# Three pairs of output blocks by seven products in steps 17 and 18 of an mLSTM and FFN kernel

## The chip, the cores and the metric

The kernel runs on one core of one Trainium2 chip, in f32 throughout. The metric is the device time of one execution in microseconds; lower is better. The engines are named as in the profile: PE (TensorE, matmul), PEld (TensorE's weight load), DVE (VectorE), ACT (ScalarE), POOL (GpSimd) and SP (SyncE, which issues most DMAs).

## The reference

An mLSTM cell runs over 768 time steps for 4 batches and 8 heads of 40; its output, as 3072 tokens of 320, goes through a multiplicative FFN:

```python
# cell, per time step t
C = f_stab * C + i_stab * outer(vt, kt);  n = f_stab * n + i_stab * kt
y[t] = sigmoid(o_gate[t]) * (C @ qt) / max(abs(n . qt), 1)
# FFN on x = y as (3072, 320)
a = x @ w1                  # 320 x 1024
b = x @ w2
out = ((a * b) @ w3) @ w_out   # 1024 x 1024, 1024 x 320
```

## The kernel before, in words

**Tiles.** The cell is computed in 24 units of 128 time steps of one batch: unit n is chunk n // 4 of batch n % 4. Four units (one chunk of all batches) make a token group of 512 tokens, six groups in all. The two last weights are folded once into one, w3 @ w_out, kept in `w3o` (128 x 8 x 320); `w3_mm` does this in eight parts ("wp" in the profile), called by `fold`. Their factors pass through `raw`, `w3` and `w3T` buffers and `wo`. After the fold, the memory of `wo` serves as `aside`.

**The FFN's first products** give `ab`, the product of x @ w1 and x @ w2, turned, 128 x 8 x 256 for each half group; six such tiles rotate. Groups 0 to 2 use the plain form (`up`, `up_rest`). Groups 3 to 5 use seven products where a 2 x 2 split of the matrices needs eight (`up_by_seven`, L676): it works on sums of weights (`weight_sums`, L659, four 128x512 operations on POOL for each of w1 and w2, into `raw` buffers) and sums of tokens (`token_sums`, L669, four 128x256 operations on DVE into a `w3T` buffer), keeps partial results in `aside`, and has POOL add and multiply.

**The FFN's last product** gives the output, 128 tokens by 320 a block, 24 blocks in all. The plain form (`ffn_out`, L741) takes 8 products of 320 columns a block. The form by seven (`out_by_seven`, L780) takes two blocks, a pair: 7 x 4 products of 160 columns, on four sums of `ab` (`ab_sums`, L771, four 128x512 operations on DVE) and four sums of the folded weight (`out_weight_sums`, L756, four 128x640 operations on POOL). Its results `p15`, `p67`, `p23` and `p4` are put together by one ACT copy and five DVE additions (L797 to L805). In the profile the products are "po" (or "cell", x32 or x16, where `ffn_out` borrows cell banks in steps 19 to 24) for the plain form and "o" for the form by seven. PE splits each f32 product in two instructions.

**The order** is written out in one loop over 32 steps (L828). Step s does, in this order: DMAs of later units' inputs on SP; the first decay of the state and the doubling of y's last columns (`twice`) on POOL; `fold`; products of `up_by_seven`; `weights(s + 1)` and `out_gate(s)` on ACT (steps 16 to 23); plain output blocks (L883 to L887); products of `up`; then `quarter_work`, the cell's own PE work, which finishes unit s - 1 and starts unit s ("cell" rows x128); then, on DVE, `x_turn` (from step 17 on: a unit's y is written to DRAM by `send` and read back by `get_back`) and `turn(s + 1)` (keys and queries turned by DVE), and on ACT `shift(s + 1)`; then `weighted` and `masks` of the next unit on POOL. Each engine works through its own instructions in the order in which they are written. Matmul results rotate through four PSUM banks of tag "m", so that a product that takes a bank waits until the engine that reads the bank's former result is through.

How much of the FFN each step does is set by lists: `n_down` (L818) says how many plain output blocks a step takes from `downs` (L812), `n_seven` how many parts of `up_by_seven` (one in each of steps 19 to 30), `n_out` how many pairs by seven (five, from step 27 on). In the kernel before, 14 blocks are plain: two in each of steps 16 to 20 and one in each of steps 21 to 24. `weight_sums` stands at the end of steps 15 and 16 (L988), the token sums of group 3 at the end of DVE's work in step 17 (L953), and the sums of the folded weight in steps 24 and 25 (L941), after the cell.

Of the kernel before, what the change touches and what calls it, by code (L numbers as in the profile page):

```python
# [8 lines left out]
FP = mybir.dt.float32  # L9
U32 = mybir.dt.uint32  # L10
AF = mybir.ActivationFunctionType
OP = mybir.AluOpType
# [4 lines left out]
def kernel(  # L17
# [26 lines left out]
    nc = tc.nc  # L44

    B, H, S, D = q.shape
    L = 64
    P = 128
    NT = S // L
    NT2 = S // P  # L50
    NU = NT2 * B
# [3 lines left out]
    DM = H * D  # L55
    BH = B * H
    DFF = moe_w1.shape[1]
    FO = DFF // P
    KF = DM // P
    REM = DM - KF * P  # L60
    GT = B
    TG = GT * P
    NG = NU // GT

    const = ctx.enter_context(tc.tile_pool(name="const", bufs=1))
    wst = ctx.enter_context(tc.tile_pool(name="wst", bufs=2))
    io = ctx.enter_context(tc.tile_pool(name="io", bufs=3))
# [42 lines left out]
    q_all = const.tile([P, NBQ * H * DP], FP, name="q_all")  # L110
    qbuf = [q_all[:, i * H * DP:(i + 1) * H * DP].rearrange("p (h d) -> p h d", d=DP) for i in range(NBQ)]
    kbuf = [const.tile([P, H, DP], FP, name=f"kbuf{i}") for i in range(NB)]
    v_all = const.tile([P, NBV * H * D1], FP, name="v_all")
# [9 lines left out]
    NY = 15  # L123
    KC = KF + 1
# [50 lines left out]
    CW = 512  # L175
# [79 lines left out]
    def fold():  # L255
        while ready_w3:
            w3_mm(ready_w3.pop(0))
        ready_w3.extend(turned_w3)
        turned_w3.clear()
# [11 lines left out]
    def out_gate(n):  # L271
        nc.scalar.activation(out=o_t[n], in_=o_t[n], func=AF.Tanh, scale=0.5)
# [27 lines left out]
    def weights(n):  # L300
        c, b = divmod(n, B)
        src = weights_tile(n) if n else spread(n)
        pw = weights_tile(n)
        for h in range(H):
            nc.scalar.activation(out=pw[:, h, :], in_=src[:, h, :], func=AF.Exp, bias=aT[:, c, b * H + h:b * H + h + 1])  # L305

    def masks(n):
        pw = weights_tile(n)
        for r in halves:
            nc.gpsimd.affine_select(out=pw[r], in_=pw[r], compare_op=OP.is_ge, fill=0.0, base=0,  # L310
                                    pattern=[[0, H], [1, L]], channel_multiplier=-1)
# [347 lines left out]
    def weight_sums(j):  # L659

        mem = [wst.tile([128, CW, 2], U32, name="raw", tag="raw", bufs=4).rearrange("p n two -> p (n two)").bitcast(FP)
               for _ in range(2)]
        S1, S2, S3, S4 = S_t[j] = [m[:, i * CW:(i + 1) * CW] for m in mem for i in range(2)]
        (A11, A21), (A12, A22) = ([(w1, w2)[j][:, cc, i * CW:(i + 1) * CW] for i in range(2)] for cc in range(KF))
        for dst, p, q, op in ((S1, A21, A22, OP.add), (S2, S1, A11, OP.subtract), (S3, A11, A21, OP.subtract),
                              (S4, A12, S2, OP.subtract)):
            nc.gpsimd.tensor_tensor(out=dst, in0=p, in1=q, op=op)

    def token_sums(gr):  # L669
        mem = wst.tile([128, FO, 128], FP, name="w3T", tag="w3T").rearrange("p k c -> p (k c)")  # L670
        T1, T2, T3, T4 = T_t[gr] = [mem[:, i * TH:(i + 1) * TH] for i in range(4)]
        (B11, B12), (B21, B22) = ([x_t[gr][:, cc, i * TH:(i + 1) * TH] for i in range(2)] for cc in range(KF))
        for dst, p, q in ((T1, B12, B11), (T2, B22, T1), (T3, B22, B12), (T4, B21, T2)):
            nc.vector.tensor_tensor(out=dst, in0=p, in1=q, op=OP.subtract)

    def up_by_seven(gr, f, bank, aside_by):  # L676

# [75 lines left out]

    KH, NH = FO // 2, DM // 2

    def out_weight_sums():  # L756

        T_o.extend(m[:, i * KH * NH:(i + 1) * KH * NH].rearrange("p (f n) -> p f n", n=NH)
                   for m, i in ((v_all, 0), (gates, 0), (gates, 1), (q_all, 0)))
        (B11, B12), (B21, B22) = ([w3o[:, k * KH:(k + 1) * KH, i * NH:(i + 1) * NH] for i in range(2)] for k in range(2))  # L760
        T1, T2, T3, T4 = T_o
        for dst, p, q in ((T1, B12, B11), (T2, B22, T1), (T3, B22, B12), (T4, B21, T2)):
            yield nc.gpsimd.tensor_tensor(out=dst, in0=p, in1=q, op=OP.subtract)

    T_o, S_o = [], {}
    wsums = out_weight_sums()

    def quarters_of_ab(gr, j):
        return [[ab_t[gr][j][:, k * KH:(k + 1) * KH, t * P:(t + 1) * P] for k in range(2)] for t in range(2)]

    def ab_sums(gr, j):  # L771
        mem = [t.rearrange("p h d -> p (h d)") if j == 0 else io.tile([P, H, L], FP, name="pw", tag="pw", bufs=5)
               .rearrange("p h t -> p (h t)") for t in kbuf]
        S1, S2, S3, S4 = S_o[gr, j] = [t.rearrange("p (f t) -> p f t", t=P) for t in mem]
        (A11, A12), (A21, A22) = quarters_of_ab(gr, j)
        for dst, p, q, op in ((S1, A21, A22, OP.add), (S2, S1, A11, OP.subtract), (S3, A11, A21, OP.subtract),
                              (S4, A12, S2, OP.subtract)):
            nc.vector.tensor_tensor(out=dst, in0=p, in1=q, op=op)  # L778

    def out_by_seven(gr, j, sums=None):  # L780


        (A11, A12), (A21, A22) = quarters_of_ab(gr, j)
        S1, S2, S3, S4 = S_o[gr, j]
        (B11, B12), (B21, B22) = ([w3o[:, k * KH:(k + 1) * KH, i * NH:(i + 1) * NH] for i in range(2)] for k in range(2))
        T1, T2, T3, T4 = T_o
        o2 = (v_all, q_all)[j][:, 2 * DM:4 * DM].rearrange("p (i n) -> p i n", n=NH)

        def products(pairs, name):
            po = mps([P, len(pairs), NH], name)  # L790
            for i, (a, b) in enumerate(pairs):
                for f in range(KH):
                    mm(po[:, i], a[:, f, :], b[:, f, :], start=(i == f == 0), stop=(i == len(pairs) - 1 and f == KH - 1))
            return po

        p15 = products(((A11, B11), (S1, T1)), "o15")
        nc.scalar.copy(out=o2[:, 0:4:3], in_=p15)  # L797
        p67 = products(((S2, T2), (S3, T3)), "o67")
        p23 = products(((A12, B21), (S4, B22)), "o23")
        p4 = products(((A22, T4),), "o4")  # L800
        for i in range(2):
            nc.vector.tensor_tensor(out=o2[:, 1 + i], in0=p67[:, i], in1=o2[:, i], op=OP.add)
        nc.vector.tensor_tensor(out=o2[:, 1:4:2], in0=o2[:, 1:3], in1=o2[:, 3:4].to_broadcast([P, 2, NH]), op=OP.add)
        nc.vector.tensor_tensor(out=o2[:, 0:2], in0=p23, in1=o2[:, 0:2], op=OP.add)
        nc.vector.tensor_tensor(out=o2[:, 2:3], in0=p4, in1=o2[:, 2:3], op=OP.add)  # L805
        for t in range(2):
            t0 = (2 * j + t) * S + gr * P
            nc.scalar.dma_start(out=out[t0:t0 + P, :], in_=o2[:, 2 * t:2 * t + 2].rearrange("p i n -> p (i n)"))

    ups = [(gr, [f, f + 1], slice(j * 2 * P, (j + 1) * 2 * P)) for gr in range(3) for j in range(2)  # L810
           for f in range(0, FO, 2)]
    downs = [(gr, j) for gr in range(NG) for j in range(GT)][:14]  # L812
    outs = [(gr, j) for gr in range(3, NG) for j in range(2)][1:]
    summed = list(outs)
    sevens = [(gr, f) for gr in range(3, NG) for f in range(FH)]
    n_up = [0] * 2 + [1] * 4 + [2] * 10 + [0] * 16
    n_seven = [0] * 19 + [1] * 12 + [0]
    n_down = [0] * 16 + [2] * 5 + [1] * 4 + [0] * 7  # L818
    n_out = [0] * 27 + [1, 0, 1, 0, 3]
    w12 = [("w12", i, part) for part in range(3) for i in range(2 * KF + 1)]  # L820
    todo = w12[5:] + [("wo", i, 0) for i in range(FO)] + [("w3", ko, part) for ko in range(FO) for part in range(2)]
# [6 lines left out]
    for s in range(len(n_up)):  # L828
# [30 lines left out]
        if NY <= s - 2 < NU:  # L859
            get_back(s - 2)  # L860
        fold()
        if s >= len(n_up) - 2:
            ab_sums(*summed.pop(0))
        def pairs():
# [8 lines left out]
        if n_seven[s]:  # L873
# [2 lines left out]
            if s <= NU:  # L876
                seven[0]()
            seven[1]()
        if NY < s < NU:
            if s < NU - 1:  # L880
                weights(s + 1)
            out_gate(s)
# [55 lines left out]
        with tc.issue_after(gated.ins) if gated else nullcontext():  # L938
            if seven:
                seven[3]()  # L940
            for _ in range({NU: 1, NU + 1: 3}.get(s, 0)):  # L941
                next(wsums)
            if s == NU + 1:
                ab_sums(*summed.pop(0))
            if NY <= s - 2 < NU:
                x_turn(s - 2)
            for n in () if s == 1 else (s + 2,) if s < B else (s + 2, s + 3) if s == B else (s + 3,):
                if n < N_U and s != B:
                    rows_of_u(n)
            if N_DVE <= s + 1 < NU:  # L950
                shift(s + 1)
                gated = turn(s + 1)
            if s - 2 in range(4 * GT - 1, NU, GT):  # L953
                token_sums((s - 2) // GT)
            if s < len(n_up) - 2 and n_out[s + 1] and s > NU + 2:
                ab_sums(*summed.pop(0))
        if s == 0:
            weighted(1)
            weights(1)
            masks(1)  # L960
            gate_cols(g, gT, nc.scalar.copy)
# [15 lines left out]
        if s < NU:  # L977
            if 0 < s < NU - 1 and s != 2:
                if s != 1:
                    weighted(s + 1)  # L980
                if s <= NY:
                    weights(s + 1)
                if 2 < s < N_DVE:
                    twice(s - 1)
                masks(s + 1)
            if s != 2 and s <= NY:
                out_gate(s)
        if s in (NY, NY + 1):  # L988
            weight_sums(s - NY)
        if s == B:  # L990
            nc.gpsimd.memset(gates[RG:P, 0:5 * TC], 0.0)
            for i, r in enumerate(third):
# [46 lines left out]
```

## Time and profile before

| what | value |
|---|---|
| median of 3 runs | 423.42 us (421.75 to 424.37) |
| the profiled execution's own time | 422.84 us |
| its span, first to last instruction | 421.1 us |
| mean granted clock of TensorE | 1.000 |
| step 16 on PE: two plain blocks, cell, transpose | 205.50 to 216.46 |
| step 17: two plain blocks, cell | 216.46 to 226.95 |
| step 18: two plain blocks, cell | 226.95 to 237.63 |
| step 19: a part by seven with two plain blocks, cell | 237.63 to 256.08 |
| step 20: the same | 256.08 to 274.55 |
| step 21: a part by seven with one plain block, cell | 274.55 to 288.68 |
| POOL's weight sums | 206.4 to 211.4 and 221.3 to 226.3 |

Times inside the profile are microseconds from the span's start. The steps' limits are where PE's products change in the chain of work that ended last. A line of the timeline or the chain gives the start, the length, the engine or line, what is written and what is read, and xN, the number of instructions taken together; "idle before" names how long the engine stood still and who released it.

### The profile page before, as it was taken

How to read it: one execution, taken by the hardware profiler on the slowest of the kernel's cores; microseconds unless marked ns; L12 is line 12 of the kernel's file. 1: busy time of each engine (PE TensorE's matmuls, PEld its weight loads, DVE VectorE, ACT ScalarE, POOL GpSimd, SP SyncE). 2: the span in 40 equal slices, each digit the busy share in tenths (PEclk: the TensorE clock that was granted, in tenths of full speed). 3: DMA queues.
4: the chain of work that ended last, by engine and by line, in shares of the span. 5: the costliest groups of instructions: out<-in, count | busy, mean ns of one | idle time of the engine just before them, and what ended most of it. 6: DMA issues, size and time to landing. Idle time of an engine off the chain costs nothing.

```text
span 421.1 us, 12970 instructions
## 1 busy us (share of the span) xinstructions
PE 410.5 (97%) x5279; PEld 332.3 (79%) x5279; DVE 292.9 (70%) x561; ACT 183.8 (44%) x526; POOL 172.3 (41%) x229
## 2 busy tenths in 40 slices
PE   7999999999999999999999999999999999999997
PEld 4768688888778868878677878788778778888896
DVE  6767967668977856867445637387776698575972
ACT  4777756558552753752755235154322210111000
POOL 4533873442311312312647333466454486542100
PEclk9999999999999999999999999999999999999999
DMA  7989986889985575941517781733321110000001
GB/s 187 226 163 200 185 189 125 192 183 197 197 194 130 110 171 144 158 85 37 100 41 164 161 151 58 146 70 79 65 55 29 28 38 15 20 0 33 2 31 62
DMA packets 125290, 46.54 MB, mean 111 GB/s; under 512 B 104816, under 2 KB 116400, under 8 KB 125232
## 3 DMA queue, kind: packets, MB, share of 16 engines
q1 hardware_dynamic: 121632, 41.70, 48.5%
q10 hardware_dynamic: 3600, 4.03, 2.7%
q8 instruction: 41, 0.67, 0.7%
q14 instruction: 17, 0.14, 0.1%
HBM read 39.91 MB, written 5.80 MB: 109 GB/s over the span
## 4 chain that ended last, share of the span: by engine, by line
PE 85%; DVE 5%; DMA 3%; SPq 3%; issue 2%; ACT 2%; POOL 0%; DVEq 0%; POOLq 0%
PE cell L92 22%; PE pa L92 21%; PE pb L92 14%; PE wp L92 8%; PE o L92 8%; PE po L92 6%; PE p L92 3%; DMA o_in<-in_o_gate_dram 2%; SPq L136 2%; PE px L95 1%; PE pt L95 1%; DVE pw L778 1%; DMA w3o<-in_moe_w_dram 1%; SPq L186 1%; DVE ab L692 1%
## 5 line engine op out<-in xcount | busy, mean ns | idle before, releaser
L337 POOL TENSOR_TENSOR state<-state,decay 128x164 f32<-128x164 f32 x40 | 22.7, 567 | 128.9 <-DVE state L406 122.9
L92 PE MATMUL pa<-xT,w 128*128 128x256 f32 x240 | 60.7, 383 | 0.0
L92 PEld LDWEIGHTS pa<-xT,w 128*128 128x128 f32 x240 | 44.3, 190 | 6.7 <-POOL w L202 0.4
L305 ACT ACTIVATE pw<-pw,aT 128x64 f32<-128x64 f32 x184 | 46.4, 337 | 2.4 <-DVE pw L297 2.0
L92 PE MATMUL pb<-xT,w 128*128 128x256 f32 x192 | 45.9, 380 | 0.8 <-POOL w L202 0.8
L737 POOL TENSOR_TENSOR ab<-ab,a_sb 128x512 f32<-128x512 f32 x22 | 29.4, 1357 | 31.3 <-DVE ab L692 31.3
L92 PEld LDWEIGHTS pb<-xT,w 128*128 128x128 f32 x192 | 36.3, 190 | 6.4 <-POOL w L202 1.6
L647 DVE TENSOR_TENSOR ab<-pb,a_sb 128x512 f32<-128x512 f32 x24 | 16.5, 689 | 33.8 <-ACT a_sb L646 33.7
L719 POOL TENSOR_TENSOR wo<-wo 128x512 f32<-128x512 f32 x22 | 27.4, 1267 | 28.5 <-DVE wo L694 28.5
L92 PE MATMUL pa<-xT,wr 64*64 64x256 f32 x384 | 37.0, 386 | 0.2 <-POOL wr L202 0.2
L92 PE MATMUL pb<-xT,wr 64*64 64x256 f32 x384 | 36.4, 380 | 0.0
L310 POOL TENSOR_SCALAR_AFFINE_SELECT pw<-pw 64x512 f32<-64x512 f32 x48 | 33.3, 693 | 7.0 <-ACT pw L305 5.5
L646 ACT ACTIVATE a_sb<-pa 128x512 f32<-128x512 f32 x24 | 14.3, 596 | 49.7 <-PE pb L92 49.6
L92 PE MATMUL wp<-wo,w3T 128*128 128x320 f32 x128 | 35.6, 432 | 0.0
L92 PE MATMUL cell<-w3o,ab 128*128 128x320 f32 x128 | 35.4, 432 | 0.0
L92 PEld LDWEIGHTS cell<-w3o,ab 128*128 128x128 f32 x128 | 24.3, 190 | 9.5
L92 PEld LDWEIGHTS wp<-wo,w3T 128*128 128x128 f32 x128 | 23.8, 190 | 9.0
L92 PEld LDWEIGHTS pa<-xT,wr 64*64 64x64 f32 x384 | 18.9, 132 | 15.1 <-issue 8.4
L434 ACT COPY h<-cell 64x164 f32<-64x164 f32 x56 | 16.2, 290 | 31.8 <-DVE y L427 31.3
L694 DVE SCALAR_TENSOR_TENSOR a_sb<-pa,wo 128x512 f32<-128x512 f32 x12 | 8.3, 688 | 31.3 <-PE pa L92 31.3
L92 PE MATMUL po<-w3o,ab 128*128 128x320 f32 x96 | 26.4, 434 | 0.0
L92 PEld LDWEIGHTS po<-w3o,ab 128*128 128x128 f32 x96 | 18.1, 190 | 7.3
(187 smaller groups left out, 883.1 us busy)
## 6 DMA issues: line engine op xcount, KB each, us to landing
raw<-in_moe_w_dram SPq DMA_DIRECT2D x64, 128.0 KB, 3.1
kbuf<-in_k_dram SPq DMA_DIRECT2D x24, 160.0 KB, 4.4
v_all<-in_v_dram SPq DMA_DIRECT2D x24, 160.0 KB, 4.7
o_in<-in_o_gate_dram SPq DMA_DIRECT2D x24, 160.0 KB, 4.8
pw<-U_d SPq DMA_DIRECT2D x28, 128.0 KB, 3.7
raw<-in_moe_w_out_dram SPq DMA_DIRECT2D x8, 320.0 KB, 3.7
out_dram<-o_sb ACTq DMA_DIRECT2D x14, 160.0 KB, 2.3
yb<-y_d SPq DMA_DIRECT2D x36, 48.0 KB, 2.6
```

What stands on the lines that cost most here:

```text
L92: in_order(nc.tensor.matmul(out, lhsT=lhsT, rhs=rhs, start=start, stop=stop))
L95: in_order(nc.tensor.transpose(out, in_, ident[0:n, 0:n]))
L136: nc.sync.dma_start(out=dst, in_=rows(src, n))
L305: nc.scalar.activation(out=pw[:, h, :], in_=src[:, h, :], func=AF.Exp, bias=aT[:, c, b * H + h:b * H + h + 1])
L310: nc.gpsimd.affine_select(out=pw[r], in_=pw[r], compare_op=OP.is_ge, fill=0.0, base=0, pattern=[[0, H], [1, L]], channel_multiplier=-1)
L337: nc.gpsimd.tensor_tensor(out=new, in0=old, op=OP.mult, in1=decay[:, b * NP:(b + 1) * NP, 2 * c + x:2 * c + x + 1] .to_broadcast([P, NP, D1]))
L434: nc.scalar.copy(out=h[halves[x], 0:H // 2] if x == e else h[halves[x], H // 2:H], in_=ph[x][halves[e]])
L646: nc.scalar.mul(out=a_sb, in_=pa, mul=UP ** -2)
L647: nc.vector.tensor_tensor(out=ab_t[gr][j][:, fs[0]:fs[-1] + 1, t0:t0 + a_sb.shape[-1]], in0=pb, in1=a_sb, op=OP.mult)
L694: nc.vector.scalar_tensor_tensor(out=out, in0=p, scalar=UP ** -2, in1=q, op0=OP.mult, op1=OP.add)
L719: aside_by.tensor_tensor(out=kept[j][:, 1:4:2], in0=kept[j][:, 1:3], in1=kept[j][:, 3:4].to_broadcast([128, 2, TH]), op=OP.add)
L737: aside_by.tensor_tensor(out=t[:, f:FO:FH, :], in0=t[:, f:FO:FH, :], in1=a, op=OP.mult)
```

## The change

Six of the plain blocks become three pairs by seven: pair (0, 1), which is the second half of group 0, and pair (1, 0) in step 17, pair (1, 1) in step 18. `downs` holds the other eight: two in step 16 and one in each of steps 19 to 24. For these pairs the sums of the folded weight are made a first time in step 16, in `aside`; the sums of `ab` are made on DVE in step 16 (for (0, 1)), at the start of step 17 (for (1, 0)) and between the two pairs (for (1, 1)), in buffers that are free at that time. The output rows lie in `o_sb` or `w3` buffers, so each row is copied and added apart, and the output DMAs are collected and issued on ACT behind the cell's work (`leave`). The two sets of `weight_sums` go to the end of step 14 and into step 15; the token sums of group 3 go to POOL, behind the masks of step 17.

```diff
-    def token_sums(gr):
+    def token_sums(gr, by=nc.vector):
...
-            nc.vector.tensor_tensor(out=dst, in0=p, in1=q, op=OP.subtract)
+            by.tensor_tensor(out=dst, in0=p, in1=q, op=OP.subtract)
...
-    def ab_sums(gr, j):
-        mem = [t.rearrange("p h d -> p (h d)") if j == 0 else io.tile([P, H, L], FP, name="pw", tag="pw", bufs=5)
-               .rearrange("p h t -> p (h t)") for t in kbuf]
+    def ab_sums(gr, j, mem=None):
+        mem = mem or [t.rearrange("p h d -> p (h d)") if j == 0 else io.tile([P, H, L], FP, name="pw", tag="pw", bufs=5)
+                      .rearrange("p h t -> p (h t)") for t in kbuf]
...
-        nc.scalar.copy(out=o2[:, 0:4:3], in_=p15)
+        if whole:
+            nc.scalar.copy(out=o2[:, 0:4:3], in_=p15)
+        for i in () if whole else range(2):
+            nc.scalar.copy(out=o[3 * i], in_=p15[:, i])
...
+            nc.vector.tensor_tensor(out=o[1 + i], in0=p67[:, i], in1=o[i], op=OP.add)
+        if whole:
+            nc.vector.tensor_tensor(out=o2[:, 1:4:2], in0=o2[:, 1:3], in1=o2[:, 3:4].to_broadcast([P, 2, NH]), op=OP.add)
+        for p, q in () if whole else ((1, 1), (3, 2)):
+            nc.vector.tensor_tensor(out=o[p], in0=o[q], in1=o[3], op=OP.add)
+        nc.vector.tensor_tensor(out=rows[0], in0=p23.rearrange("p i n -> p (i n)"), in1=rows[0], op=OP.add)
+        nc.vector.tensor_tensor(out=o[2], in0=p4[:, 0], in1=o[2], op=OP.add)
         for t in range(2):
             t0 = (2 * j + t) * S + gr * P
-            nc.scalar.dma_start(out=out[t0:t0 + P, :], in_=o2[:, 2 * t:2 * t + 2].rearrange("p i n -> p (i n)"))
+            leaving.append((out[t0:t0 + P, :], rows[t]))
+        if whole:
+            leave()
+
+    leaving = []
+
+    def leave():
+        while leaving:
+            dst, src = leaving.pop(0)
+            nc.scalar.dma_start(out=dst, in_=src)
...
-    downs = [(gr, j) for gr in range(NG) for j in range(GT)][:14]
+    downs = [(0, 0), (0, 1)] + [(2, j) for j in range(GT)] + [(3, 0), (3, 1)]
+    pairs_by = {17: [(0, 1), (1, 0)], 18: [(1, 1)]}
...
-    n_down = [0] * 16 + [2] * 5 + [1] * 4 + [0] * 7
+    n_down = [0] * 16 + [2] + [0] * 2 + [1] * 6 + [0] * 7
...
         fold()
+        if s == 15:
+            weight_sums(1)
+        if s == 16:
+            for _ in out_weight_sums([(aside, i) for i in range(4)]):
+                pass
+            ab_sums(0, 1, [ffn.tile([128, 2, TH], FP, name="a_sb", tag="a_sb").rearrange("p i t -> p (i t)") for _ in range(2)] +
+                    [wst.tile([128, CW], FP, name="w3", tag="w3") for _ in range(2)])
+        if s == 17:
+            ab_sums(1, 0, [x_t[2][:, i] for i in range(KC)] +
+                    [wst.tile([128, FO, 128], FP, name="w3T", tag="w3T")[:, 0:4].rearrange("p k c -> p (k c)")])
+        if s in pairs_by:
+            weights(s + 1)
+            out_gate(s)
+        for x in pairs_by.get(s, ()):
+            if x == (1, 0):
+                mem = ffn.tile([128, FO, TH], FP, name="ab", tag="ab", bufs=6)
+                ab_sums(1, 1, [mem[:, i * 2:i * 2 + 2].rearrange("p i t -> p (i t)") for i in range(4)])
+            out_by_seven(*x, [wst.tile([128, CW], FP, name="w3", tag="w3")[:, 0:DM] if x == (1, 0) else
+                              ffn.tile([P, DM], FP, name="o_sb", tag="o_sb", bufs=2) for _ in range(2)])
...
-        if NY < s < NU:
+        if NY < s < NU and s not in pairs_by:
...
-            if s - 2 in range(4 * GT - 1, NU, GT):
+            if s - 2 in range(5 * GT - 1, NU, GT):
                 token_sums((s - 2) // GT)
...
+        leave()
...
                 masks(s + 1)
+                if s == 4 * GT + 1:
+                    token_sums(3, nc.gpsimd)
...
-        if s in (NY, NY + 1):
-            weight_sums(s - NY)
+        if s == 14:
+            weight_sums(0)
```

More of the change, by code (lines that the diff above doesn't have):

```diff
@@ L754, with out_weight_sums @@
     KH, NH = FO // 2, DM // 2
-    def out_weight_sums():
-        T_o.extend(m[:, i * KH * NH:(i + 1) * KH * NH].rearrange("p (f n) -> p f n", n=NH)
-                   for m, i in ((v_all, 0), (gates, 0), (gates, 1), (q_all, 0)))
+    def out_weight_sums(places):
         (B11, B12), (B21, B22) = ([w3o[:, k * KH:(k + 1) * KH, i * NH:(i + 1) * NH] for i in range(2)] for k in range(2))
-        T1, T2, T3, T4 = T_o
+        T1, T2, T3, T4 = T_o[:] = [m[:, i * KH * NH:(i + 1) * KH * NH].rearrange("p (f n) -> p f n", n=NH) for m, i in places]
         for dst, p, q in ((T1, B12, B11), (T2, B22, T1), (T3, B22, B12), (T4, B21, T2)):
@@ L765 @@
     T_o, S_o = [], {}
-    wsums = out_weight_sums()
+    wsums = out_weight_sums(((v_all, 0), (gates, 0), (gates, 1), (q_all, 0)))
     def quarters_of_ab(gr, j):
         return [[ab_t[gr][j][:, k * KH:(k + 1) * KH, t * P:(t + 1) * P] for k in range(2)] for t in range(2)]
-    def ab_sums(gr, j):
-        mem = [t.rearrange("p h d -> p (h d)") if j == 0 else io.tile([P, H, L], FP, name="pw", tag="pw", bufs=5)
-               .rearrange("p h t -> p (h t)") for t in kbuf]
+    def ab_sums(gr, j, mem=None):
+        mem = mem or [t.rearrange("p h d -> p (h d)") if j == 0 else io.tile([P, H, L], FP, name="pw", tag="pw", bufs=5)
+                      .rearrange("p h t -> p (h t)") for t in kbuf]
         S1, S2, S3, S4 = S_o[gr, j] = [t.rearrange("p (f t) -> p f t", t=P) for t in mem]
@@ L778, in ab_sums, with out_by_seven @@
             nc.vector.tensor_tensor(out=dst, in0=p, in1=q, op=op)
-    def out_by_seven(gr, j, sums=None):
+    def out_by_seven(gr, j, rows=None):
         (A11, A12), (A21, A22) = quarters_of_ab(gr, j)
@@ L787, in out_by_seven @@
         o2 = (v_all, q_all)[j][:, 2 * DM:4 * DM].rearrange("p (i n) -> p i n", n=NH)
+        whole, rows = not rows, rows or [o2[:, 2 * t:2 * t + 2].rearrange("p i n -> p (i n)") for t in range(2)]
+        o = [t.rearrange("p (i n) -> p i n", n=NH)[:, i] for t in rows for i in range(2)]
         def products(pairs, name):
@@ L801, in out_by_seven @@
         for i in range(2):
[L802 to L805, printed above, removed]
+            nc.vector.tensor_tensor(out=o[1 + i], in0=p67[:, i], in1=o[i], op=OP.add)
[5 more added lines that the diff above has]
+        nc.vector.tensor_tensor(out=o[2], in0=p4[:, 0], in1=o[2], op=OP.add)
         for t in range(2):
             t0 = (2 * j + t) * S + gr * P
-            nc.scalar.dma_start(out=out[t0:t0 + P, :], in_=o2[:, 2 * t:2 * t + 2].rearrange("p i n -> p (i n)"))
+            leaving.append((out[t0:t0 + P, :], rows[t]))
[6 more added lines that the diff above has]
+            nc.scalar.dma_start(out=dst, in_=src)
     ups = [(gr, [f, f + 1], slice(j * 2 * P, (j + 1) * 2 * P)) for gr in range(3) for j in range(2)
            for f in range(0, FO, 2)]
-    downs = [(gr, j) for gr in range(NG) for j in range(GT)][:14]
+    downs = [(0, 0), (0, 1)] + [(2, j) for j in range(GT)] + [(3, 0), (3, 1)]
+    pairs_by = {17: [(0, 1), (1, 0)], 18: [(1, 1)]}
     outs = [(gr, j) for gr in range(3, NG) for j in range(2)][1:]
```

## The prediction

> **What bounds the kernel now.** I read the page's busy shares first, then the chain of work that ended last in order of time, then a table of the engines by stage, and last the single instructions of VectorE and GpSimd where the change puts new work.
>
> ```profile
> PE 410.5 (97%) x5279; PEld 332.3 (79%) x5279; DVE 292.9 (70%) x561; ACT 183.8 (44%) x526; POOL 172.3 (41%) x229
> ```
>
> PE is busy nearly all the time. Only what shortens PE's own stream, or makes PE wait, can move the end. The chain around the change, and one pair of last products by seven near the end:
>
> ```profile
> 205.50 8.61 PE po L92 x32
> 214.11 1.87 PE cell L92 x128
> 215.98 0.48 PE px L95 x3
> 216.46 8.62 PE po L92 x32
> 225.08 1.87 PE cell L92 x128
> 226.95 8.81 PE po L92 x32
> 235.76 1.87 PE cell L92 x128
> ...
> 240.42 12.07 PE cell L92 x48
> ...
> 258.87 12.10 PE cell L92 x48
> ...
> 277.34 7.76 PE cell L92 x32
> ...
> 374.82 7.61 PE o L92 x56
> ```
>
> Columns are start, length, what, instructions. A product of f32 is two PE instructions, so one plain block (8 products of 320 columns) is x16 and two are the x32 of "po". Steps 16, 17 and 18 are the three "po" rows, each ahead of its "cell" row. The x48 rows are the shared products of step 19 and of step 20 (x16) with two plain blocks (x32). The x32 row is step 21, where one block takes the place of two. "o x56" is one pair by seven: 28 products of 160 columns. From 205 to 290 every piece of this chain is PE, without a gap.
>
> ```profile
> 237.63:256.08 18.45, 18.45 (x221) 14.38 (x221) 9.68 (x19) 6.45 (x21) 5.80 (x7) 1.00 0.72 147
> 274.55:288.68 14.13, 14.13 (x189) 11.31 (x189) 10.68 (x20) 6.22 (x20) 7.91 (x9) 1.00 0.43 88
> ```
>
> Step 19 and step 21 (length, then busy us of PE, PEld, DVE, ACT, POOL; clock, DMA share, GB/s): in both PE is busy to the last hundredth, and the granted clock is 1.00.
>
> **The change part by part, PE first.** Six plain blocks leave steps 17 to 20 and come back as three pairs by seven.
> - Step 17: 8.62 goes, two pairs come, 2 x 7.61 = 15.22. That is +6.60.
> - Step 18: 8.81 goes; it is 8.62 and 0.19 lost on the way in from "cell", with no "px" between. The pair follows "cell" too: 7.61 + 0.19 = 7.80. That is -1.01.
> - Step 19: 12.07 becomes the 7.76 of step 21, -4.31. Step 20: 12.10 becomes 7.76, -4.34.
> - Sum: 6.60 - 1.01 - 4.31 - 4.34 = **-3.06 us**. (Check: a plain pair is 8.62, one by seven 7.61, 1.01 apart, and there are three.) The last three pairs, 23.03 for x168 with the drain, give 7.68 each, so by them the gain would be 2.8.
>
> A rule of the Trainium skill speaks against this gain. The row first: each weight load is 190 ns and a matmul of 160 columns 299 ns, yet the 56 took 7.61 us, 136 ns each, so loads run under matmuls. "TensorE: Matmul & The Clock Gate", Part 3, The mechanism, says that a weight load overlaps with matmuls in flight only when it goes to other rows of the array; all of these use all 128 rows. By the rule the 24 more loads of each pair by seven would be added; by the row they cost nothing. The time it gives is the last rival.
>
> **VectorE, 12 new sums of ab (128x512).** One is 0.68 alone, four in a row take 2.53 (399.65 to 402.18). Beside GpSimd they stretch:
>
> ```profile
> 342.38 1.64 DVE L778 TENSOR_TENSOR pw<-pw,ab 128x512 f32<-128x512 f32 x1
> 343.94 2.03 DVE L778 TENSOR_TENSOR pw<-ab 128x512 f32<-128x512 f32 x1
> 345.89 2.02 DVE L778 TENSOR_TENSOR pw<-ab,pw 128x512 f32<-128x512 f32 x1
> ```
>
> ```profile
> 343.43 1.99 POOL L763 TENSOR_TENSOR gates<-w3o,v_all 128x640 f32<-128x640 f32 x1
> 345.38 1.99 POOL L763 TENSOR_TENSOR gates<-w3o 128x640 f32<-128x640 f32 x1
> ```
>
> So four cost 2.5 us alone and 8 us beside four GpSimd operations of 1.99. I take 8 for step 16, where both sets of four run, and 2.5 for each set of step 17, where GpSimd has only one decay of 0.46.
> - Step 16, pair (0,1): VectorE is idle for 8.91 us before its multiply at 215.25. That covers the four sums, even stretched, but with little over.
> - Step 17: VectorE ends its turn for step 17 at about 222.0. Then sums of (1,0) to 224.5, six output additions of (0,1) (2 x 0.33 out of PSUM, 2 x 0.32, 0.49, 0.32; 2.1) to 226.6, sums of (1,1) to 229.1, six additions of (1,0) from 229.1, the last of them released by PE at 231.7. PE's second pair starts at 224.07. It needs the first sum 1.1 later (225.2; ready 222.7) and the bank that the first two additions free at 226.25 (free at 225.2). Slack 1.0. "cell" starts at 231.7 and its first multiply is due 1.2 later, so the additions are out of the way.
> - Step 18: from its first multiply to the end of the turn VectorE took 226.22 to 233.6 before, 7.4. Now 232.9 to 240.3, and PE needs the turned k about 1 us into "cell", 242.2. Slack 1.9. The additions of (1,1) then end at 242.3, just before the multiply due at 242.5; cover is the 1 us or so until PE reuses the cell's banks in step 19.
> - Token sums of group 3 leave VectorE's step 18 tail (4 x 0.42): nothing gained, PE did not wait for it.
>
> **GpSimd.** Two sets of weight sums (4 x 1.27 each) move, from after steps 15 and 16 to step 14's end and into step 15, ahead of step 15's decays, of the doubled y column that PE's transpose needs, and of the mask.
>
> The first set starts at 191.0 and, with up to 0.4 for each VectorE conversion beside it, ends at 196 to 197.5; decay and copy follow by 198.7 (PE needs the copy at 200.64). The second ends at 202.1 to 203.6, while the decay behind it ran at 202.67: up to 1.4 late, and so are state, y and the turn for step 16, which PE uses at 215. The four sums of w_out (128x640) are new: they need the last fold's copy (205.98), run from 207.0 or, late, 207.8, at 1.59 (1.27 x 640/512, an estimate) to 1.99 each, and end by 215.8. PE needs the first at 217.5, the last at 223. Queued behind is the decay for which VectorE asks at 217.9. Token sums of group 3 (between the 0.46 of a 128x164 and the 1.27 of a 128x512; I take 0.7, nearest 0.73 for 128x328): after the mask of step 18, 238.8 to 241.6; PE's first use is 243.5, and the decay that waits behind them is due at about 245. Cover 1.9.
>
> **ScalarE and the queues.** Each pair adds two copies of about 0.3 and moves two output DMAs (0.35 to issue) behind the cell's copies and shift. In step 17 the ScalarE queue carries four: 236.0 to 237.4, then 8 exponentials and the gate to 239.9, then the copies for (1,1), whose buffer an output transfer (2.3 to land) frees at 238.6. VectorE reaches the additions at 240.3, so 0.2 may be lost there, not on PE. SP's list is unchanged; its write of y(16) shifts with the cell, and the read back lands 10.9 after y as before (230.9 to 241.8): x_turn then waits 1 us more at the start of step 19, and in step 21 VectorE still stands idle for 2.44 us, waiting for PE, after the work that this delays (at 286.24).
>
> No wait reaches PE in this sum, so the profiled execution, 422.84 (span 421.1 and 1.74 around it), would be 419.8. It lies 0.58 under the median of 423.42, so against the median **420.3**.
>
> **The rivals.**
> 1. *VectorE is late in step 16 and PE waits in step 17.* Step 16's sums can end after 215.25: from 208 at 2.0 each they end at 216.0. The slack of 1.0 takes that up. Were GpSimd's list 1 to 3 us later still, PE would lose 1 to 2.5: 421.3 to 422.8, say 421.8. For: the stretched rows. Against: PE's x56 of the first pair is a cushion of 7.6.
> 2. *Other side: VectorE becomes the bound of step 17 because its eight sums are stretched there too.* At 2.02 the eight take 16.2; with 6.75 for the cell and 4.2 for the additions it is 27.1, against 15.22 + 1.87 = 17.1 on PE: 10.0 lost, 430.3. It decides against the change when it eats the 3.06, at 20.2 on VectorE, or 1.15 us a sum. Against: GpSimd's own list is empty there, its weight sums being gone from 221 to 226.
> 3. *Steps 19 and 20 do not shrink, because transfers or VectorE set them.* Then +6.60 - 1.01: 429.0. Against: step 21 has the same work and 14.13, with PE full.
> 4. *More than forecast.* PE has one gap of 0.78 at 199.66 in step 15, put down to "issue". Without it, 419.5.
> 5. *Weight loads add up.* 24 more at 190 ns is 4.56 a pair, 13.7 for three; with the sum's 3.06, 434.1. Against: the 7.61 of x56. That is the page's rule; the trace disagrees with it.
>
> **How the numbers follow.** Forecast 0.66, rival 1 0.18, rival 2 0.05, rival 3 0.03, rival 4 0.07, rival 5 0.01. The likeliest is 420.3; the two prices of a pair (2.8 or 3.06) and the spread of the runs before (421.75 to 424.37, about 1.3 either side; a median of three moves less, some 0.8) make its own range 419.4 to 421.4. To 8 in 10 it takes in rivals 1 and 4: 418.8 to 423.2. About 1% (4.2 us) is what a measurement of this kernel can tell from no change. The forecast is 0.7% faster, so most of it is "within 1%": 0.56 of the 0.66, rival 1 and 0.03 of rival 4, together 0.77. Faster by over 1%, under 419.2, needs the other 0.10 of the forecast (a low median) and 0.04 of rival 4: 0.14. Slower by over 1%, over 427.7: rivals 2, 3 and 5: 0.09.
>
> **What would show it.** In the chain, step 17 with x112 of "o" in 15.2 and no gap, step 18 with x56 in 7.8, steps 19 and 20 with 7.8 where 12.1 stood. VectorE's sums of step 16 at up to 2 us, of step 17 at 0.68. GpSimd's token sums at about 0.7. Wrong would be: PE idle before the second pair's third product (rival 1) or through step 17 (rival 2), steps 19 or 20 longer than 14.5 (rival 3), x56 longer than 7.8 (rival 5).

## The result, and the profile after

The changed kernel takes 420.56 us (median of 6 runs, 419.23 to 421.11) against 423.93 us before (6 runs in the same comparison). The ratio is 0.9924, with a 95% interval of 0.9901 to 0.9948: faster by 0.5 to 1.0%. The forecast was 420.3. The profiled execution took 419.57 us with a span of 417.7; the forecast for it was 419.8.

The busy shares, from the page of the changed kernel:

```profile
PE 407.5 (98%) x5351; PEld 337.3 (81%) x5351; DVE 311.5 (75%) x587; ACT 182.9 (44%) x526; POOL 183.3 (44%) x237
```

PE lost 3.0 us of busy time although it issues 72 more matmuls; DVE gained 18.6 and POOL 11.0, and neither shows in the end. The chain that ended last, in order of time (start, length, what):

```profile
205.12 8.61 PE po L92 x32
213.73 1.87 PE cell L92 x128
215.60 0.48 PE px L95 x3
216.08 15.21 PE o L92 x112
231.29 1.87 PE cell L92 x128
233.16 7.80 PE o L92 x56
240.97 1.87 PE cell L92 x128
...
245.62 7.76 PE cell L92 x32
...
259.77 7.79 PE cell L92 x32
```

These are steps 16 to 20. Against the rows shown of before: step 17 has 15.21 where 8.62 stood, step 18 has 7.80 for 8.81, and steps 19 and 20 have 7.76 and 7.79 for 12.07 and 12.10. The sum is +6.59 - 1.01 - 4.31 - 4.31 = -3.04 us. No other engine stands between the pieces. Step 19 is now as long as step 21 (length, busy us of PE, PEld, DVE, ACT, POOL):

```profile
242.84:256.98 14.14, 14.14 (x205) 11.33 (x205) 9.70 (x19) 6.08 (x20) 5.80 (x7) 1.00 0.81 161
271.14:285.28 14.14, 14.14 (x190) 11.34 (x189) 10.69 (x20) 6.22 (x20) 7.92 (x9) 1.00 0.59 121
```

Where VectorE has its new work, the timeline of steps 16 and 17 reads so:

```profile
207.47 0.69 DVE L776 TENSOR_TENSOR a_sb<-ab 128x512 f32<-128x512 f32 x1
208.19 1.92 DVE L776 TENSOR_TENSOR a_sb<-a_sb,ab 128x512 f32<-128x512 f32 x1
210.04 2.02 DVE L776 TENSOR_TENSOR w<-ab 128x512 f32<-128x512 f32 x1
211.98 2.02 DVE L776 TENSOR_TENSOR w<-ab,a_sb 128x512 f32<-128x512 f32 x1
214.87 0.50 DVE L427 TENSOR_TENSOR y<-cell,gT 128x328 f32<-128x328 f32 x1 [0.87 <-PE cell L92]
...
223.33 0.69 DVE L776 TENSOR_TENSOR w3T<-ab,xT 128x512 f32<-128x512 f32 x1
223.93 0.68 DVE L805 TENSOR_TENSOR o_sb<-o,o_sb 128x160 f32<-128x160 f32 x2
```

PE's products two to four of the second pair are one line of its timeline:

```profile
224.61 3.42 PE L92 MATMUL o<-wo,xT 128*128 128x160 f32 x24
```

The sums of step 16 stretch to 2.02 beside GpSimd's four sums and still end 0.87 before the cell's multiply (L427), which waits for PE. The sums of step 17 have GpSimd idle beside them and take 0.69. The first two additions (L805) free a PSUM bank at 224.61; PE takes that bank for the second pair's third product at 225.70 (the second starts at 224.61, and products of this pair follow each other by 1.09). The slack is 1.09 us, the narrowest place that was found in the change.

Profiled executions, one for each kernel, differ by up to 2.2 us before they reach step 16 (204.95 to 207.19 over all kernels here), in gaps that are there with and without the change. For the experiments I therefore also give the **tail**, the time from PE's first product of step 16 to the end of the span (a line of PE's timeline, taken from the span): 215.8 before, 212.7 after, 3.0 less. The tail leaves out steps 14 and 15, where the weight sums now lie. From the fold's first product in step 14 to step 16 PE takes 20.63 before, 19.79 after and 19.60 to 20.69 over all kernels, and what is over 19.6 goes with one gap in step 15 that comes with and without the moves.

### The profile page after: what moved, and what is told of

Read it like the earlier page. It is cut to its first block, busy times and chain, and to the rows that moved or that the text cites. A ratio compares the mean times of both kernels' runs of the same rounds, so it can differ in the third digit from the quotient of the medians.

```text
span 417.7 us, 13157 instructions
## 1 busy us (share of the span) xinstructions
PE 407.5 (98%) x5351; PEld 337.3 (81%) x5351; DVE 311.5 (75%) x587; ACT 182.9 (44%) x526; POOL 183.3 (44%) x237
## 4 chain that ended last, share of the span: by engine, by line
PE 85%; DVE 4%; DMA 3%; SPq 3%; issue 2%; ACT 1%; POOL 0%; DVEq 0%; ACTq 0%; POOLq 0%
PE pa L92 21%; PE cell L92 20%; PE pb L92 14%; PE o L92 14%; PE wp L92 8%; PE p L92 3%; PE po L92 2%; DMA o_in<-in_o_gate_dram 2%; DMA w3o<-in_moe_w_dram 1%; SPq L136 1%; SPq L186 1%; PE px L95 1%; PE pt L95 1%; DVE pw L776 1%; DVE ab L692 1%
## 5 line engine op out<-in xcount | busy, mean ns | idle before, releaser
L92 PE MATMUL cell<-w3o,ab 128*128 128x320 f32 x96 | 26.8, 432 | 0.0
L92 PEld LDWEIGHTS cell<-w3o,ab 128*128 128x128 f32 x96 | 18.3, 190 | 6.9
L92 PEld LDWEIGHTS pb<-xT,wr 64*64 64x64 f32 x384 | 20.1, 133 | 3.0
L92 PE MATMUL o<-w3o,ab 128*128 128x160 f32 x136 | 21.5, 302 | 0.5 <-DVE wo L694 0.5
```

Source lines behind the costliest of these rows:

```text
L92: in_order(nc.tensor.matmul(out, lhsT=lhsT, rhs=rhs, start=start, stop=stop))
```

## The experiments

The theory: the gain is PE's shorter stream, 1.01 us for each pair by seven; the new sums and the moved ones cost nothing as long as the bank at 225.70 is freed in time, and the moves of GpSimd's work are what frees it in time. The rival: the moves themselves, or the order of the work, take waits away, and the products by seven matter less.

| kernel | median us | ratio to before (95%) | tail | tail less the changed kernel's |
|---|---|---|---|---|
| changed kernel | 420.56 | 0.9924 (0.9901 to 0.9948) | 212.7 | 0 |
| moves alone | 423.92 | 1.0025 (1.0006 to 1.0043) | 215.8 | +3.0 |
| third pair plain | 421.83 | 0.9947 (0.9925 to 0.9970) | 213.7 | +1.0 |
| no sums | 421.89 | 0.9955 (0.9927 to 0.9983) | 212.7 | 0.0 |
| all moves undone | 428.08 | 1.0107 (1.0089 to 1.0125) | 220.9 | +8.2 |
| weight sums moved back | 427.82 | 1.0099 (1.0064 to 1.0134) | 220.3 | +7.5 |
| token sums moved back | 420.73 | 0.9923 (0.9896 to 0.9949) | 212.9 | +0.1 |
| four more additions | 422.44 | 0.9977 (0.9960 to 0.9994) | 214.8 | +2.0 |
| twelve more additions | 428.43 | 1.0125 (1.0074 to 1.0177) | 220.0 | +7.3 |
| one pair, then two | 424.61 | 1.0030 (1.0008 to 1.0052) | 217.8 | +5.1 |
| a fourth pair | 421.98 | 0.9956 (0.9932 to 0.9979) | 213.6 | +0.9 |

**The moves alone**, on the kernel before (the lines that let GpSimd do the token sums are left out, as are unchanged lines, at each "..."):

```diff
...
+        if s == 15:
+            weight_sums(1)
...
+                if s == 4 * GT + 1:
+                    token_sums(3, nc.gpsimd)
...
-        if s in (NY, NY + 1):
-            weight_sums(s - NY)
+        if s == 14:
+            weight_sums(0)
```

> The kernel before with nothing but the moves: weight sums at the end of step 14 and in step 15, token sums of group 3 on GpSimd; all 14 blocks stay plain. Theory (the gain is PE's shorter stream, 1.01 us a pair, and the moves only make room): no change, within 0.5 us of before, steps 16 to 18 on PE 10.96, 10.5 and 10.7 as before. Rival (the moves themselves take waits away): 1 to 3 us faster than before.

The tail is that of before to the tenth (215.8), so the moves gain nothing, and the rival falls. The time is 0.06 to 0.43% longer than before, and that excess goes with the granted clock. Eight of the twelve runs have a mean clock of 0.995 or 0.996, against nine of 29 below 0.999 before. The other four took 423.39 to 423.70, and before's other twenty have a median of 423.45. In the profiled execution the clock was 0.58 and 0.57 in the stretches 22 to 24 and 24 to 26 us, long before anything that was moved. Why it fell more often here is not shown.

**The third pair plain again**, in the changed kernel:

```diff
...
-    pairs_by = {17: [(0, 1), (1, 0)], 18: [(1, 1)]}
+    pairs_by = {17: [(0, 1), (1, 0)], }
...
-    n_down = [0] * 16 + [2] + [0] * 2 + [1] * 6 + [0] * 7
+    n_down = [0] * 16 + [2, 0, 2] + [1] * 6 + [0] * 7
...
```

> The changed kernel with the third pair, (1,1), back to two plain blocks in step 18, and without its sums. Theory: 8.81 in place of 7.80 in step 18, so 1.0 us over the changed kernel, and nothing else moves. Rival (the gain does not go by the pair): no change, or more than 2 us.

Step 18 reads 8.81 in the chain where the changed kernel has 7.80, and the tail is 1.0 longer. This pair is worth the 1.01 of the sum; the other two were not taken back one by one.

**Without the twelve sums of ab:**

```diff
+        if gr < 3:
+            S_o[gr, j] = A21, A22, A11, A12
+            return
```

> The changed kernel without the twelve new sums of ab: the products of the three pairs read quarters of ab in place of sums, the rest is unchanged. Theory (all twelve lie beside PE's work): same time as the changed kernel within 0.3 us in the chain, 15.21 and 7.80 for the pairs. Rival (they cost on the path): 0.5 to 2 us faster than the changed kernel.

The chain has 15.22 and 7.80, and the tail is the same to the tenth. The median is higher than the changed kernel's (ratio to before 0.9927 to 0.9983) although work was taken away. This too goes with the clock: four of the nine runs have a mean of 0.988 to 0.996 and took 422.38 to 424.69, and the other five have a median of 420.31, where the changed kernel's five runs of 0.999 or 1.000 have 420.37. All twelve sums are hidden.

**The weight sums and the token sums moved back**, both, and then each alone. The edit for the weight sums (the token sums go back by the list of steps and the call that the change had moved):

```diff
-        if s == 15:
-            weight_sums(1)
...
-        if s == 14:
-            weight_sums(0)
+        if s in (NY, NY + 1):
+            weight_sums(s - NY)
```

> The changed kernel with the moves undone: weight sums again at the end of steps 15 and 16, token sums of group 3 on VectorE. Theory: PE waits in step 17, since GpSimd's second set of weight sums then runs beside VectorE's sums for pair (1,0), which stretch from 0.68 to 1.3 or more, and the bank that the first additions free comes about 3 us late: a gap of 2 to 4 us on PE ahead of the second pair's third product, and a time near that of before. Rival (the place of GpSimd's work does not matter): 420.5, no gap.

> The changed kernel with the two sets of weight sums again at the end of steps 15 and 16, the token sums of group 3 left on GpSimd. Theory (the weight sums alone make the wait that was seen with all moves undone): a gap of 4 to 5 us on PE ahead of the second pair's third product, a granted clock near 0.5 behind it, and 427 to 429 in all. Rival (the two moves are needed together): no gap above 1 us.

> The changed kernel with the token sums of group 3 on VectorE again, at the end of its step 17 work, and the weight sums left where the change puts them. Theory (PE's wait depends on the weight sums, not on these): four sums of 0.42 put the additions of (1,1) and the multiply behind them about 1.5 us later, within the 1 us or so of cover at the cell's banks in step 19, so 0 to 0.6 us over the changed kernel. Rival (VectorE is at its limit in step 18): 1.5 us over.

With the token sums back on VectorE the tail is 0.1 longer. The weight sums are what matters: with them back the change is a loss of 0.6 to 1.3% against before, as the expectation for them alone said. With both back, the expectation was too low: the gap is 4.25, a second wait of 0.67 stands ahead of the second product, and the time is 1% over before, not near it. VectorE's timeline in steps 16 and 17 of the kernel with the weight sums back, and GpSimd's in step 17:

```profile
216.91 1.57 DVE L447 TENSOR_TENSOR h<-y,h 128x328 f32<-128x328 f32 x1 [0.18 <-ACT h L434]
...
218.75 1.16 DVE L451 SCALAR_TENSOR_TENSOR den<-den 128x8 f32<-128x8 f32 x1
...
223.74 1.31 DVE L776 TENSOR_TENSOR xT<-ab 128x512 f32<-128x512 f32 x1
225.08 1.64 DVE L776 TENSOR_TENSOR xT<-xT,ab 128x512 f32<-128x512 f32 x1
226.65 1.75 DVE L776 TENSOR_TENSOR xT<-ab 128x512 f32<-128x512 f32 x1
228.32 1.75 DVE L776 TENSOR_TENSOR w3T<-ab,xT 128x512 f32<-128x512 f32 x1
229.98 0.67 DVE L805 TENSOR_TENSOR o_sb<-o,o_sb 128x160 f32<-128x160 f32 x2
```

```profile
223.22 1.27 POOL L667 TENSOR_TENSOR raw<-w 128x512 f32<-128x512 f32 x1
224.58 1.60 POOL L667 TENSOR_TENSOR raw<-raw,w 128x512 f32<-128x512 f32 x1
226.14 1.71 POOL L667 TENSOR_TENSOR raw<-w 128x512 f32<-128x512 f32 x1
227.81 1.71 POOL L667 TENSOR_TENSOR raw<-w,raw 128x512 f32<-128x512 f32 x1
```

Each of VectorE's sums is as long as the GpSimd operation beside it, to 0.04. GpSimd's own go from 1.27 to 1.71. Counted from the second pair's first product on PE, the bank comes free 5.8 later than in the changed kernel (at 230.65, after 6.85 instead of 1.09). The stretched sums are 3.7 of this. The other 2.1 come from step 16: L447 takes 1.57 and L451 1.16, where the changed kernel has 0.50 and 0.17, because they run beside GpSimd's sums of w_out, which end at 219.88 instead of 215.40 behind the first set of weight sums. So both sets have a part; they were not put back one by one. PE stands still:

```profile
225.10 1.35 PE L92 MATMUL o<-wo,xT 128*128 128x160 f32 x8
230.71 4.63 PE L92 MATMUL o<-wo,xT 128*128 128x160 f32 x16 [4.25 <-DVE o_sb L805]
235.14 1.76 PE L92 MATMUL o<-w3o,ab 128*128 128x160 f32 x8
```

The gap is 4.25, and the 16 instructions behind it take 4.63 where they take 2.34 elsewhere. The same stretch in the table by stage (the figure after POOL's is the granted clock):

```profile
230.60:235.00 4.40, 4.29 (x16) 4.29 (x17) 3.83 (x9) 0.00 (x0) 0.00 (x0) 0.50 0.52 108
```

The clock is halved in this stretch; that adds 2.3 on the x16 and 0.5 on the next x8. Together with the gap it makes 7.05 of the 7.5. All eight runs of this kernel have a mean clock of 0.992 to 0.996.

**More work on VectorE ahead of the narrow place**, four additions and then twelve:

```diff
+        if s == 17:
+            (A11, A12), (A21, A22) = quarters_of_ab(1, 0)
+            for _ in range(4):
+                nc.vector.tensor_tensor(out=S_o[1, 0][3], in0=A12, in1=S_o[1, 0][1], op=OP.subtract)
```

> The changed kernel with four more 128x512 additions on VectorE in step 17, between the sums of (1,0) and the first output additions (the last of the sums, written again). Theory: 4 x 0.62 is 2.5 of delay against a slack of 1.25 (first two additions end at 224.61, PE takes their bank at 225.86): a gap of about 1.2 us on PE and 1.2 us more than the changed kernel. Rival (the slack is larger, other waits are met first): no gap.

> As the kernel with four more additions in step 17, but twelve: 12 x 0.62 is 7.4 of delay against a slack of 1.25: a gap of about 6.2 us on PE, 6.2 us over the changed kernel and 3 us slower than before. Rival (part of the delay is taken up elsewhere): less than 4 us over the changed kernel.

Four put the gap where it was expected, but 1.73 long instead of the 1.2 expected, and the tail is 2.0 longer:

```profile
228.87 2.44 PE L92 MATMUL o<-wo,xT 128*128 128x160 f32 x16 [1.73 <-DVE o_sb L805]
```

The four took 2.87 together. Counted from the second pair's first product, the first two output additions end 2.9 later than in the changed kernel and the third product starts 1.9 later, so the usable slack is 1.0. The granted clock stayed at 1.00, and the mean is 0.999 or 1.000 in all ten runs. Twelve took 8.7, and the wait moved: the third product waited 0.58 for ScalarE's copies and the fifth, which is the next to take a bank, 4.51 for VectorE's additions. So the third product seems to have been given another bank here; that is read from the waits alone. The clock fell to 0.50 from 236 to 239 here too. So the gap was 5.1 in place of the 6.2 that I expected, and the clock more than made up for the difference (+7.3 of tail). The rival, that part of the delay is taken up elsewhere, was right on the gap and wrong on the time.

**One pair in step 17 and two in step 18:**

```diff
-    pairs_by = {17: [(0, 1), (1, 0)], 18: [(1, 1)]}
+    pairs_by = {17: [(0, 1)], 18: [(1, 0), (1, 1)]}
```

> The changed kernel with one pair, (0,1), in step 17 and two, (1,0) and (1,1), in step 18; VectorE's sums of (1,1) move with the second pair. PE's stream is as long as in the changed kernel. Theory: VectorE then has the cell of step 17 and the turn before the additions of (1,0) and sums of (1,1), which start at about 233.4 and free the third product's bank at 236.6, where PE wants it at 235.4: a gap of about 1.2 us or a little more on PE in step 18. Rival (only PE's length counts, the place does not): the changed kernel's time within 0.3 us.

PE waits where that was expected, though for longer:

```profile
237.01 1.35 PE L92 MATMUL o<-wo,ab 128*128 128x160 f32 x8 [0.41 <-DVE ab L776]
240.73 4.10 PE L92 MATMUL o<-wo,ab 128*128 128x160 f32 x16 [2.37 <-DVE w L805]
```

The sums of (1,1) took 3.81 beside GpSimd's token sums instead of the 2.5 that I had allowed, so the gap was 2.8 in two parts and not 1.2. Behind it the granted clock was 0.50 from 242 to 244 in this execution. Out of the gap and the clock came 5.1 of tail. This execution is one of the two longest of ten (426.60); the medians are 4.1 apart (424.61 and 420.56), and the two runs with a mean clock of 1.000 took 423.73 and 423.90. So the gap alone seems to take the gain away, and the fall of the clock does not seem to come in every run (these two have no trace): the place of the pairs decides between a gain and none.

**A fourth pair by seven**, (2,0) in step 18:

```diff
-    pairs_by = {17: [(0, 1), (1, 0)], 18: [(1, 1)]}
+    pairs_by = {17: [(0, 1), (1, 0)], 18: [(1, 1), (2, 0)]}
...
-    n_down = [0] * 16 + [2] + [0] * 2 + [1] * 6 + [0] * 7
+    n_down = [0] * 16 + [2] + [0] * 3 + [1, 0, 1, 1, 1] + [0] * 7
...
```

> The changed kernel with a fourth pair, (2,0), by seven behind (1,1) in step 18, its four sums on VectorE in step 17; steps 19 and 21 then have no plain block, steps 20, 22, 23 and 24 one each. By PE's length alone 1.0 us less than the changed kernel. Theory (a pair pays only where the other engines keep up): steps 19 and 21 would be 9.8 on PE with 9.7 and 10.7 of VectorE's work in them, so PE waits 1 us or more in each, and the time is 0 to 2 us over the changed kernel. Rival (the gain goes by the pair here too): 419.6, no new gap.

Counted from the start of one cell to the next, steps 19 and 21 fall to 9.9 and 9.8, as PE's length says, and the waits that I expected there are absent. Steps 20 and 22 grow from 14.2 and 14.1 to 14.8 and 15.3, with PE waiting there (the second row lies in the cell of step 21, which this count puts into step 22):

```profile
267.44 1.99 PE L92 MATMUL cell<-w3T,raw 128*128 128x256 f32 x8 [0.30 <-DVE state L416]
286.64 0.69 PE L92 MATMUL cell<-qT,kT 40*64 40x64 f32 x32 [0.28 <-DVE wo L692]
290.85 0.70 PE L92 MATMUL cell<-xT,w 128*128 128x256 f32 x2 [0.42 <-ACT h L434]
```

VectorE was late, but a step later than I had put it; the 1.0 of PE's stream is gone and the tail is 0.9 longer than the changed kernel's. The time is in the expected 0 to 2 us over it, and the gain does not go by the pair any further.

## Why the prediction was right, point by point

- **Which engine sets the end:** right. In steps 16 to 22 the chain after is PE alone, and the twelve sums can be left out without a change of the tail.
- **The terms of PE's sum:** 15.22, 7.80, 7.76 and 7.76 forecast; 15.21, 7.80, 7.76 and 7.79 measured; -3.06 against -3.04. The lower price of a pair (2.8 for three) was not needed. 423.42 less 3.06 is 420.36, so the 420.3 is a shade low. The rest of the 3.4 by which the spans differ lies ahead of step 16 (205.34 to 204.95) and is scatter. That the median came within 0.3 us of the forecast is in part luck: the six runs spread over 1.9 us, and before itself had a median of 423.42 in the first three runs and 423.93 in the six. The gap of 0.78 in step 15 (rival 4) is down to 0.2 in this execution (step 15's cell takes 1.90 where step 14's takes 1.71). Seven of the ten experiments show 0.2 to 0.84 of it as a wait, so the change does not remove it.
- **VectorE, step 16:** the stretch to 2.02 was right, its end was mis-sized: four sums took 6.5, not 8, since the first ran alone. They ended 0.87 early where I had feared 0.75 late.
- **VectorE, steps 17 and 18:** first two additions freed the bank 1.09 ahead of PE (1.0 forecast); the experiment with four more shows 1.0 of it as usable. The turn of step 18 ended at 239.86, 2.0 ahead of its use (1.9 forecast).
- **GpSimd:** second weight sums until 203.61 (202.1 to 203.6 forecast), decay 1.3 late (up to 1.4), sums of w_out until 215.40 (215.8), token sums 0.73 each (0.7).
- **Queues:** x_turn of step 19 waited 0.77 for the read back (1 forecast), and nothing came of it.
- **The rule on weight loads** (rival 5) is out as the prediction took it: the 56 instructions of step 18 took 7.80 with their way in. The section of the Trainium skill that the prediction quotes also lets a load go ahead into a background weight buffer, so the rows contradict the one sentence, and not the whole section.
- **What failed** is the price in rival 2, a side branch that the change avoids. It took VectorE's extra time over PE's as the loss and set its break-even at 1.15 us a sum over all eight. With the weight sums back the eight took 9.1 (four stretched to 1.3 to 1.75, four in 2.6), which is 1.13 each and by its terms 20.0 on VectorE and 2.9 lost, about break-even. The tail lost 7.5. The terms left out the 2.1 of stretched cell work in step 16 and the 2.8 of the half clock behind PE's gap, which together make up the difference roughly.

## What to carry to other kernels

Where one engine is busy all the time, cost an edit by the length of that engine's stream, and then look for the one place where its cover is thinnest (here a PSUM bank freed 1 us early); that place, not the sum of the hidden work, decides whether the gain is kept. Work moved to an engine with idle time has to be placed by what runs beside it: the two sets of weight sums cost no tail in steps 14 and 15 and 7.5 us at the ends of steps 15 and 16. Price a longer wait on PE as more than its length: here 1.73 us cost about its length, and waits of 2.8 us (in two parts) and more cost more in most runs or all. Where two medians differ by less than 1%, compare the granted clocks of the runs first.

## What the runs showed of the hardware

A long wait on PE cost more than its length. After a gap of 1.73 us the granted clock stayed at 1.00. With the gap of 4.25 us it was halved, and PE worked at 0.50 for some 5 us behind it; 4.51 us, with 0.58 ahead of it, brought 0.50 for 3 us. The Trainium skill, "TensorE: Matmul & The Clock Gate", section Why this matters for your kernels, warns of idle gaps above some 3 us between bursts; the trace agrees, and shows it for a smaller gap too: 2.37 us, with 0.41 a little ahead of it, brought 0.50 from 242 to 244. Two of that kernel's ten runs kept a mean clock of 1.000, so this gap does not seem to halve the clock every time. Nor is a gap of that length always needed: in the profiled execution of the moves alone the clock was 0.58 and 0.57 from 22 to 26 us, with waits of no more than 0.38 us just ahead, and the kernel before, with the same waits there, kept 1.00. The mean clocks of the runs lie near 1.000, 0.996, 0.992 and 0.988; over a span of 425 us a step of 0.004 is 3.4 us at half clock (an estimate from these means).

VectorE's sums with two operands in SBUF last as long as the GpSimd operation beside them (0.69 alone, 1.75 beside 1.71, 2.02 beside 1.98), and GpSimd's stretch as well, from 1.27 to 1.71. By the Trainium skill, "SBUF — State Buffer", section SBUF: two separate sides, the two engines take turns at one pair of ports. The trace agrees in kind, though not to the full length: turns of 0.69 and 1.27 would need 1.96 for one operation of each (an estimate from the times alone), and in step 17 of the kernel with the weight sums back one of each took 1.67 (VectorE's start at 226.65 and 228.32, GpSimd's at 226.14 and 227.81). Additions that read PSUM and one SBUF operand did not stretch: in the changed kernel two of them at 239.67 took 0.70 beside the token sums and 0.68 at 223.93 alone, while the two behind them, with both operands in SBUF, took 1.15 instead of 0.69.
